# Top-32 attention on one core: the exponential moved ahead of the selection's end, and the threshold applied by a scaled Relu and a subtraction

## The chip, the cores and the metric

One core of a Trainium2 chip. TensorE (PE; PEld is its weight load), VectorE (DVE), ScalarE (ACT) and GpSimd (POOL) each run their own queue in order; SyncE (SP) issues the DMAs. The metric is the device time of one execution in microseconds, lower is better.

## The reference

```python
scores = scale * np.matmul(q, k.transpose(0, 1, 3, 2))          # 4 batches, 8 heads, 576 x 576, head size 64
kth = np.partition(scores, -top_k, axis=-1)[..., -top_k:-top_k + 1]   # top_k = 32
mask = scores >= kth
scores = np.where(mask, scores, -1000000000.0)
scores = scores - np.max(scores, axis=-1, keepdims=True)
attn = np.exp(scores)
attn = attn / (np.sum(attn, axis=-1, keepdims=True) + 1e-09)
return np.matmul(attn, v).astype(np.float32)
```

Each row of scores keeps its 32 largest entries. Two dense blocks follow for each batch: a token and channel mixing with cosine and sine, then a gated layer with a normalisation, all in float32 by three matmuls on split operands.

## The kernel before

**Attention.** The 4 x 4 pairs of heads are cut into 144 tiles of 128 query rows by 576 keys; two tiles make a group (G = 2), so there are 72 groups. For each tile `scores` makes the score tile in PSUM (`ps_s`, L449) and ScalarE copies it into `x` (L453; three group buffers). `topk` then works on a group on VectorE alone: four tensor_tensor steps with two tensors each (L468 max, L469 min, twice: 288 columns of both tiles, then 144) narrow the row, MAX8 at L472 takes the losers' best, and four rounds of MAX8 (L478) and MATCH_REPLACE8 (L481) give the 32 largest in `mx`. Round 0 gives the row maximum, `mx[..., 0]`; round 3 gives the 32nd, `mx[..., 31]`. A compare (L485, `flags`) records rows in which the narrowing may have lost an entry.

**The threshold.** ScalarE puts -max/8 into `cf` (L489) and |32nd| times a small number (L490), VectorE forms the threshold from it in one scalar_tensor_tensor of 128 x 2 (L491). `weigh` has ScalarE make `sg` = sign(score - threshold) (L500), then `x` = exp((score - max)/8) in place (L501), and GpSimd multiplies them into `sg` in pieces of 288 columns (L89, four for a group). TensorE transposes `sg` into `ps_t` (L511), ScalarE takes Relu of that into `ptb` (L512), which removes the negative entries, and `values` multiplies with V (`ps_v`, L522 to L536). A column of ones in V gives the row sum.

**What else runs.** From about 0 to 300 us the weights of the dense blocks are converted (VectorE L163 to L165, ScalarE, GpSimd `w_f`, `w_hi`); from about 300 us the dense blocks of batches 0 to 2 (`ps_m`, L572 to L574; their other operations go through a helper and stand at L588 or L89) are laid between the attention's instructions; the dense block of batch 3 runs after the attention's end.

**Order.** The Python loop emits `topk` of group g, then `weigh`, `transpose` and `values` of group g - 1. A scheduler that plans by priorities and its own estimates fixes the order of each engine's queue from that; buffers have fixed counts (`x` 3, `sg` 2, `mm` 1). A buffer's new writer waits for its last reader: `sg` of group g for the transposes of group g - 2.

Of the kernel before, what the change touches and what calls it, by code (L numbers as in the profile page):

```python
# [10 lines left out]
F32 = mybir.dt.float32  # L11
F32R = mybir.dt.float32r
I32 = mybir.dt.int32
AF = mybir.ActivationFunctionType
OP = mybir.AluOpType
# [1 line left out]
NEG = -3.0e38  # L17
MAGIC = 12582912.0
TURN = 6.283185
ULP = 1.25 * 2.0 ** -24  # L20
LN_EPS = 1e-6


# [1 line left out]
def sparse_attention_then_moe_kernel(  # L25
# [21 lines left out]
    B, H, D, S = qT.shape  # L47
# [4 lines left out]
    G = 2  # L52
# [38 lines left out]
    pool = Pieces()  # L91
# [244 lines left out]
    def run(exact):  # L336
# [93 lines left out]
            nc.sync.dma_start(extra[p, 0:D], v[b, 2 * j + 1, r])  # L430

        GATE = {}
        X, SG, MX, PT = {}, {}, {}, {}
        PER = NP * NT

        def scores(n):
# [17 lines left out]

        def topk(g):

            x = X[g]
            mx = att.tile([128, G, 32], F32, name="mx")
            mm = att.tile([128, G, S], F32, name="mm", bufs=1)
            if exact:  # L460
                src, mr = ([t[:, i] for i in range(G)] for t in (x, mm))
            else:


                z = att.tile([128, G, QUARTER + 16], F32, name="z", bufs=1)
                for t, lo, mid, hi, win in ((x, 0, HALF, S, mm), (mm, 0, QUARTER, HALF, z)):
                    a, b = t[:, :, lo:mid], t[:, :, mid:hi]
                    dve.tensor_tensor(win[:, :, 0:mid], a, b, op=OP.max)  # L468
                    dve.tensor_tensor(mm[:, :, mid:hi], a, b, op=OP.min)  # L469
                for k, losers in enumerate((slice(LOSERS, S), slice(QUARTER, LOSERS))):  # L470
                    for i in range(G):
                        dve.max(out=z[:, i, QUARTER + 8 * k:QUARTER + 8 * k + 8], in_=mm[:, i, losers])  # L472
                src = [z[:, i] for i in range(G)]
                mr = [mm[:, i, 0:QUARTER + 16] for i in range(G)]
            for r in range(4):
                top = [mx[:, i, 8 * r:8 * r + 8] for i in range(G)]
                for i in range(G):
                    last = dve.max(out=top[i], in_=src[i])  # L478
                if r < 3:
                    for i in range(G):  # L480
                        dve.match_replace(out=mr[i], in_to_replace=top[i], in_values=src[i], imm_value=NEG)  # L481
                    src = mr
            kth = mx[:, :, 31]
            if not exact:
                dve.tensor_tensor(flags[:, g], z[:, :, QUARTER + 7::8], mx[:, :, 31:32].to_broadcast([128, G, 2]),  # L485
                                  op=OP.is_gt)

            cf = att.tile([128, G, 3], F32, name="cf", bufs=3)
            act.activation(cf[:, :, 0], mx[:, :, 0], AF.Copy, scale=-0.125)  # L489
            act.activation(cf[:, :, 1], kth, AF.Abs, scale=ULP)  # L490
            dve.scalar_tensor_tensor(cf[:, :, 2], cf[:, :, 1], 1e-37, kth, op0=OP.max, op1=OP.subtract)  # L491
            MX[g] = cf
            GATE[g] = last.ins

        def weigh(n):
            x, cf = X[n // G][:, n % G], MX[n // G][:, n % G]
            if n % G == 0:
                SG[n // G] = att.tile([128, G, S], F32, name="sg", bufs=2)
            sg = SG[n // G][:, n % G]
            act.activation(sg, x, AF.Sign, bias=cf[:, 2:3])  # L500
            act.activation(x, x, AF.Exp, bias=cf[:, 0:1], scale=0.125)  # L501
            pool.tensor_tensor(sg, x, sg, op=OP.mult)

        def transpose(n):
            x = SG[n // G].rearrange("p i n -> p (i n)")
            pt = psum.tile([128, 5, 128], F32, name="ps_t")
            ptb = att.tile([128, 5, 128], F32, name="ptb", bufs=2)
            k = (5, 4)[n % G]
# [584 lines left out]
```

## Time and profile before

| | |
|---|---|
| median of 3 runs | 989.75 us (989.65 to 991.41) |
| the profiled execution | 992.02 us, its span 990.2 us |
| busy, share of the span | PE 88%, DVE 83%, ACT 64%, POOL 60% |
| granted TensorE clock, mean | 0.901 of 2.4 GHz |

The busy time of PE counts matmuls that overlap in the pipeline. The chain that ended last has PE on 43%, DVE on 26%, ACT on 10%, DMA on 9% and POOL on 6% of the span.

### The profile page before, as it was taken

Reading aid. Unit: us, or ns where it says so; the run is one execution under the profiler, and the core shown is the slowest. Engines: PE = TensorE matmul, PEld = TensorE weight load, DVE = VectorE, ACT = ScalarE, POOL = GpSimd, SP = SyncE. Lnnn points to the kernel's source line nnn. Section 1 sums busy time; section 2 is a strip of 40 time slices with the busy share of each in tenths; the row PEclk is TensorE's granted clock in tenths of the full one; section 3 lists DMA queues with packets and bytes.
Section 4 is the critical chain, followed back from the end, with each engine's and each line's share of the span. In section 5 each row is a group of like instructions: output and inputs, shape, how many; then the busy total and the mean of one; then the engine's idle time right before and its main releaser. Section 6 shows DMA issues by size and latency. Waiting matters only on the chain.

```text
span 990.2 us, 18081 instructions
## 1 busy us (share of the span) xinstructions
PE 867.8 (88%) x5802; PEld 797.5 (81%) x5802; DVE 823.0 (83%) x2710; ACT 638.0 (64%) x1319; POOL 598.7 (60%) x753
## 2 busy tenths in 40 slices
PE   4657686678779799989999999999989999999997
PEld 2546575667669798888889998898889998889987
DVE  6999999999998897889999998999998981363552
ACT  5566676779858566877776777777966775350121
POOL 2798876686956755594767666676584564421030
PEclk9955556679779699999999999899999999999999
DMA  7797665545817633744362753552743554441221
GB/s 218 215 305 227 215 210 179 145 145 186 261 60 199 230 95 106 229 143 126 110 206 60 229 160 78 218 129 95 205 160 91 201 188 166 191 168 62 104 85 52
DMA packets 79395, 159.78 MB, mean 161 GB/s; under 512 B 36143, under 2 KB 40239, under 8 KB 71866
## 3 DMA queue, kind: packets, MB, share of 16 engines
q1 hardware_dynamic: 79290, 158.53, 50.5%
q8 instruction: 48, 0.79, 0.3%
q14 instruction: 57, 0.47, 0.2%
HBM read 108.63 MB, written 23.32 MB: 133 GB/s over the span
## 4 chain that ended last, share of the span: by engine, by line
PE 43%; DVE 26%; ACT 10%; DMA 9%; POOL 6%; issue 4%; SPq 2%; ACTq 0%; POOLq 0%; DVEq 0%
PE ps_m L574 9%; PE ps_m L572 9%; PE ps_m L573 9%; PE ps_v L533 7%; DVE mm L469 4%; PE ps_s L449 4%; PE ps_t L511 4%; DVE mm L481 4%; DVE mx L478 4%; DVE z L472 2%; DVE mm L468 2%; DMA raw<-in_q_dram 2%; DMA q<-hi 2%; ACT sg L500 1%; POOL sg L89 1%
## 5 line engine op out<-in xcount | busy, mean ns | idle before, releaser
L89 POOL TENSOR_TENSOR sg<-x,sg 128x288 f32<-128x288 f32 x288 | 238.5, 857 | 141.0 <-ACT x L501 94.2
L511 PE MATMUL ps_t<-ident,sg 128*128 128x128 f32 x648 | 140.9, 314 | 60.7 <-POOL sg L89 37.5
L533 PE MATMUL ps_v<-vc,ptb 128*128 128x65 f32 (+1 forms) x1280 | 183.5, 281 | 4.7 <-ACT ptb L512 4.7
L533 PEld LDWEIGHTS ps_v<-vc,ptb 128*128 128x128 f32 (+1 forms) x1280 | 174.7, 206 | 13.6 <-ACT ptb L512 6.7
L511 PEld LDWEIGHTS ps_t<-ident,sg 128*128 128x128 f32 x648 | 97.8, 171 | 77.6 <-POOL sg L89 51.2
L500 ACT ACTIVATE sg<-x,cf 128x576 f32<-128x576 f32 x144 | 103.8, 768 | 44.2 <-DVE cf L491 43.3
L478 DVE MAX8 mx<-mm 128x8 f32<-128x160 f32 x432 | 118.8, 312 | 0.0
L453 ACT ACTIVATE x<-ps_s 128x576 f32<-128x576 f32 x144 | 92.6, 643 | 35.9 <-PE ps_s L449 32.3
L512 ACT ACTIVATE ptb<-ps_t 128x640 f32<-128x640 f32 (+1 forms) x144 | 92.7, 644 | 29.8 <-PE ps_t L511 28.2
L501 ACT ACTIVATE x<-x,cf 128x576 f32<-128x576 f32 x144 | 107.9, 767 | 0.1
L449 PE MATMUL ps_s<-k,q 128*128 128x288 f32 x256 | 91.3, 368 | 16.2 <-DVE q L369 8.6
L572 PE MATMUL ps_m<-w_t,zah 128*128 128x288 f32 (+2 forms) x272 | 98.9, 364 | 6.6 <-DVE F L588 4.8
L574 PE MATMUL ps_m<-w_t,zal 128*128 128x288 f32 (+2 forms) x272 | 97.5, 360 | 0.6 <-POOL zal L89 0.5
L573 PE MATMUL ps_m<-w_t,zah 128*128 128x288 f32 (+2 forms) x272 | 96.7, 356 | 0.0
L472 DVE MAX8 z<-mm 128x8 f32<-128x312 f32 (+1 forms) x288 | 89.6, 372 | 2.0
L572 PE MATMUL ps_m<-w_t,zbh 128*128 128x288 f32 x288 | 85.7, 302 | 2.3 <-DMA w_t<-d_sph 1.0
L481 DVE MATCH_REPLACE8 mm<-mx,mm 128x160 f32<-128x160 f32 x288 | 86.8, 308 | 0.0
L573 PE MATMUL ps_m<-w_t,zbh 128*128 128x288 f32 x288 | 86.2, 303 | 0.0
L574 PE MATMUL ps_m<-w_t,zbl 128*128 128x288 f32 x288 | 84.9, 302 | 1.2 <-POOL zbl L89 1.2
L449 PE MATMUL ps_s<-kl,q 128*128 128x288 f32 x256 | 82.9, 334 | 0.0
L468 DVE TENSOR_TENSOR mm<-x 128x576 f32<-128x576 f32 x72 | 67.7, 941 | 17.5 <-ACT x L453 16.4
L89 POOL TENSOR_TENSOR raw<-raw,hi 128x288 fp32r<-128x288 f32 x60 | 56.2, 956 | 40.2 <-ACT hi L393 40.0
(174 smaller groups left out, 2438.9 us busy)
## 6 DMA issues: line engine op xcount, KB each, us to landing
k<-hi SPq DMA_DIRECT2D x60, 144.0 KB, 2.5
kl<-raw SPq DMA_DIRECT2D x60, 144.0 KB, 2.6
vc<-in_v_dram SPq DMA_DIRECT2D x48, 128.0 KB, 2.9
w_t<-d_trh SPq DMA_DIRECT2D x4, 1152.0 KB
w_t<-d_trl SPq DMA_DIRECT2D x4, 1152.0 KB
out_dram<-t SPq DMA_DIRECT2D x32, 144.0 KB, 2.5
raw<-in_q_dram SPq DMA_DIRECT2D x15, 288.0 KB, 3.0
q<-hi SPq DMA_DIRECT2D x30, 144.0 KB, 3.3
```

Of the source, the lines that this page charges most:

```text
L89: nc.gpsimd.tensor_tensor(out[:, lo:hi], a[:, lo:hi], b[:, lo:hi], op=op)
L449: pe.matmul(o, q, k[:, m], start=a == 0, stop=a == len(terms) - 1)
L472: dve.max(out=z[:, i, QUARTER + 8 * k:QUARTER + 8 * k + 8], in_=mm[:, i, losers])
L478: last = dve.max(out=top[i], in_=src[i])
L481: dve.match_replace(out=mr[i], in_to_replace=top[i], in_values=src[i], imm_value=NEG)
L500: act.activation(sg, x, AF.Sign, bias=cf[:, 2:3])
L501: act.activation(x, x, AF.Exp, bias=cf[:, 0:1], scale=0.125)
L511: pe.transpose(pt[:, c, :], x[:, lo:lo + 128], ident)
L533: pe.matmul(o, pt[:, c, q], chunks[:, c, slot], start=alone and c == 0, stop=not alone and i == 1 and c == 3)
L572: pe.matmul(out, ah, bh, start=first, stop=False)
L573: pe.matmul(out, ah, bl, start=False, stop=False)
L574: pe.matmul(out, al, bh, start=False, stop=last)
```

## The change

Two things move. The exponential no longer waits for the 32nd largest: after round 0 of `topk`, ScalarE forms `most` = -max/8 and writes exp((score - max)/8) of both tiles into a new tile `e`, which takes the two buffers that `sg` had. After round 3 ScalarE alone forms `kth` = 2^64 times the 32nd; `weigh` then makes `x` = relu(2^64 (32nd - score)) in place, and GpSimd subtracts it from `e`, in the same pieces as the product before. An entry below the 32nd becomes hugely negative and is removed by the Relu behind the transposes, as before. The sign and VectorE's scalar_tensor_tensor at L491 are gone, and the small Abs on ScalarE with them.

```diff
@@ topk
                     last = dve.max(out=top[i], in_=src[i])
+                if r == 0:
+                    most = att.tile([128, G], F32, name="most", bufs=3)
+                    e = att.tile([128, G, S], F32, name="e", tag="sg", bufs=2)
+                    act.activation(most, mx[:, :, 0], AF.Copy, scale=-0.125)
+                    for i in range(G):
+                        act.activation(e[:, i], x[:, i], AF.Exp, bias=most[:, i:i + 1], scale=0.125)
+                    E[g] = e
...
-            cf = att.tile([128, G, 3], F32, name="cf", bufs=3)
-            act.activation(cf[:, :, 0], mx[:, :, 0], AF.Copy, scale=-0.125)
-            act.activation(cf[:, :, 1], kth, AF.Abs, scale=ULP)
-            dve.scalar_tensor_tensor(cf[:, :, 2], cf[:, :, 1], 1e-37, kth, op0=OP.max, op1=OP.subtract)
-            MX[g] = cf
             GATE[g] = last.ins
+            MX[g] = att.tile([128, G], F32, name="kth", bufs=3)
+            act.activation(MX[g], mx[:, :, 31], AF.Copy, scale=LACK)
@@ weigh
-            act.activation(sg, x, AF.Sign, bias=cf[:, 2:3])
-            act.activation(x, x, AF.Exp, bias=cf[:, 0:1], scale=0.125)
-            pool.tensor_tensor(sg, x, sg, op=OP.mult)
+            act.activation(x, x, AF.Relu, bias=kth, scale=-LACK)
+            pool.tensor_tensor(e, e, x, op=OP.subtract)
```

The scheduler lays the queues anew. In the changed file L483 is `most`, L485 the exponential, L496 `kth`, L502 the Relu; VectorE's steps stand at L469, L470, L473, L479, L489 and L492, the transposes at L512 and their Relu at L513.

VectorE, group 12, from its round 3 to the next group's narrowing (`w_f` is a weight's conversion). Before:

```order
L478 MAX mx<-mm 128x8 x2
L163 TENSOR_SCALAR w_f<-w_raw 128x512
L468 TENSOR_TENSOR mm<-x 128x2x288
L469 TENSOR_TENSOR mm<-x 128x2x288
L485 TENSOR_TENSOR flags<-z,mx 128x4
L164 SCALAR_TENSOR_TENSOR w_f<-w_raw,w_f 128x512
L491 SCALAR_TENSOR_TENSOR cf<-cf,mx 128x2
L468 TENSOR_TENSOR z<-mm 128x2x144
```

After:

```order
L479 MAX mx<-mm 128x8 x2
L163 TENSOR_SCALAR w_f<-w_raw 128x512
L469 TENSOR_TENSOR mm<-x 128x2x288
L470 TENSOR_TENSOR mm<-x 128x2x288
L492 TENSOR_TENSOR flags<-z,mx 128x4
L164 SCALAR_TENSOR_TENSOR w_f<-w_raw,w_f 128x512
L469 TENSOR_TENSOR z<-mm 128x2x144
```

One instruction is gone, which stood behind two tensor_tensor steps of the next group; the rest kept its place.

ScalarE, the same group 12, from the row maximum on. Before:

```order
L489 ACTIVATE cf<-mx 128x2
L393 ACTIVATE hi<-raw 128x576
L490 ACTIVATE cf<-mx 128x2
L512 ACTIVATE ptb<-ps_t 128x640
L453 ACTIVATE x<-ps_s 128x576
L500 ACTIVATE sg<-x,cf 128x576 x2
L501 ACTIVATE x<-x,cf 128x576
L166 ACTIVATE w_raw<-w_raw 128x512
L211 ACTIVATE w_f<-w_f 128x512
L501 ACTIVATE x<-x,cf 128x576
```

After:

```order
L483 ACTIVATE most<-mx 128x2
L485 ACTIVATE e<-x,most 128x576 x2
L496 ACTIVATE kth<-mx 128x2
L502 ACTIVATE x<-x,kth 128x576 x2
L513 ACTIVATE ptb<-ps_t 128x512
L453 ACTIVATE x<-ps_s 128x576
```

Both exponentials now stand between round 0 and round 3, and both Relus directly behind `kth`.

ScalarE in the stage with dense work (`zah` and L588/L589 are the dense block's), from group 49's row maximum on. Before:

```order
L489 ACTIVATE cf<-mx 128x2
L512 ACTIVATE ptb<-ps_t 128x640
L588 ACTIVATE zah<-F 128x288
L453 ACTIVATE x<-ps_s 128x576
L490 ACTIVATE cf<-mx 128x2
L393 ACTIVATE hi<-raw 128x576
L588 ACTIVATE zah<-F 128x288
L500 ACTIVATE sg<-x,cf 128x576
L512 ACTIVATE ptb<-ps_t 128x512
L500 ACTIVATE sg<-x,cf 128x576
```

After (the two Relus that come first are group 48's):

```order
L483 ACTIVATE most<-mx 128x2
L502 ACTIVATE x<-x,kth 128x576 x2
L453 ACTIVATE x<-ps_s 128x576
L589 ACTIVATE zah<-F 128x288
L496 ACTIVATE kth<-mx 128x2
L547 ACTIVATE xr<-ps_v 128x130
L513 ACTIVATE ptb<-ps_t 128x640
L589 ACTIVATE zah<-F 128x288
L453 ACTIVATE x<-ps_s 128x576
L589 ACTIVATE zah<-F 128x288
L513 ACTIVATE ptb<-ps_t 128x512
L485 ACTIVATE e<-x,most 128x576 x2
```

Here the exponentials stand behind `kth`, after the copy-out of the transposes that free their buffer, and group 48's Relus stand behind group 49's row maximum.

## Rows read from the trace of the kernel before

**Rows 1.** Stretches: length, busy us (count) of PE, PEld, DVE, ACT, POOL; clock, DMA, GB/s.

```profile
0.00:300.00 300.00, 211.29 (x1064) 181.36 (x1065) 284.31 (x861) 208.51 (x415) 212.89 (x270) 0.72 0.64 197
300.00:820.00 520.00, 495.35 (x3635) 465.30 (x3634) 470.44 (x1675) 381.54 (x805) 344.05 (x430) 0.97 0.49 154
820.00:990.20 170.20, 161.20 (x1107) 150.81 (x1105) 68.26 (x175) 47.90 (x100) 41.77 (x54) 0.99 0.33 121
```

**Rows 2.** The page's chain that ended last, by engine.

```profile
PE 43%; DVE 26%; ACT 10%; DMA 9%; POOL 6%; issue 4%; SPq 2%; ACTq 0%; POOLq 0%; DVEq 0%
```

**Rows 3.** L491 alone in the same stretches: busy us (count), clock, DMA share, GB/s.

```profile
0.00:300.00 300.00, 8.05 (x23) 0.72 0.64 197
300.00:820.00 520.00, 13.63 (x49) 0.97 0.49 154
```

**Rows 4.** Groups by line and form: count, busy us, mean ns, idle before, its releasers.

```profile
L491 DVE SCALAR_TENSOR_TENSOR cf<-cf,mx 128x2 f32<-128x2 f32 x72 | 21.7, 301 | 2.8 <-ACT cf L490 2.6
L501 ACT ACTIVATE x<-x,cf 128x576 f32<-128x576 f32 x144 | 107.9, 767 | 0.1
L500 ACT ACTIVATE sg<-x,cf 128x576 f32<-128x576 f32 x144 | 103.8, 768 | 44.2 <-DVE cf L491 43.3 <-PE ps_t L511 0.5
L89 POOL TENSOR_TENSOR sg<-x,sg 128x288 f32<-128x288 f32 x288 | 238.5, 857 | 141.0 <-ACT x L501 94.2 <-issue 36.6 <-PE ps_s L449 7.7
L89 POOL TENSOR_TENSOR pl<-F,ph 128x288 fp32r<-128x288 f32 x52 | 44.0, 858 | 44.8 <-ACT ph L588 27.2 <-DVE ph L588 17.2 <-issue 0.2
```

**Rows 5.** Timeline around 109 us, all engines: start us, us, engine, line, operation, operands.

```profile
109.37 2.65 POOL L89 TENSOR_TENSOR raw<-raw,hi 128x288 fp32r<-128x288 f32 x2
...
111.29 0.75 DVE L491 SCALAR_TENSOR_TENSOR cf<-cf,mx 128x2 f32<-128x2 f32 x1
...
111.96 0.45 DVE L468 TENSOR_TENSOR z<-mm 128x288 f32<-128x288 f32 x1
```

**Rows 6.** VectorE's timeline near 540 us, the same columns.

```profile
537.50 1.36 DVE L468 TENSOR_TENSOR mm<-x 128x576 f32<-128x576 f32 x1
...
540.05 0.15 DVE L491 SCALAR_TENSOR_TENSOR cf<-cf,mx 128x2 f32<-128x2 f32 x1
540.12 0.45 DVE L468 TENSOR_TENSOR z<-mm 128x288 f32<-128x288 f32 x1
```

**Rows 7.** Timeline of an early group, all engines.

```profile
93.84 1.12 PE L511 MATMUL ps_t<-ident,sg 128*128 128x128 f32 x4 [0.79 <-ACT ptb L512]
...
102.91 0.54 DVE L478 MAX8 mx<-z 128x8 f32<-128x160 f32 x2
...
112.07 1.44 ACT L500 ACTIVATE sg<-x,cf 128x576 f32<-128x576 f32 x2 [1.19 <-DVE cf L491]
```

**Rows 8.** Timeline of a group in the stage with dense work, all engines.

```profile
568.22 0.54 DVE L478 MAX8 mx<-z 128x8 f32<-128x160 f32 x2
...
572.34 0.60 PE L511 MATMUL ps_t<-ident,sg 128*128 128x128 f32 x4
...
575.09 1.45 ACT L500 ACTIVATE sg<-x,cf 128x576 f32<-128x576 f32 x2 [0.24 <-DVE cf L491]
...
577.81 2.34 POOL L89 TENSOR_TENSOR sg<-x,sg 128x288 f32<-128x288 f32 x3 [0.74 <-ACT x L501]
```

**Rows 9.** Waits (us in total, times, longest): ACT, whole span; PE, 550 to 820 us.

```profile
ACT cf L490 <- DVE mx L478: 22.6, 21, 2.7
...
PE ps_t L511 <- POOL sg L89: 2.6, 3, 1.7
```

**Rows 10.** L468, then L469, from 0 to 300 us: busy us, count.

```profile
0.00:300.00 300.00, 39.01 (x49) 0.72 0.64 197
...
0.00:300.00 300.00, 41.16 (x48) 0.72 0.64 197
```

**Rows 11.** VectorE's timeline: an early wide step and a late narrow one.

```profile
130.28 0.75 DVE L468 TENSOR_TENSOR mm<-x 128x576 f32<-128x576 f32 x1
...
575.45 0.95 DVE L469 TENSOR_TENSOR mm<-mm 128x288 f32<-128x288 f32 x1
```

More of the change, by code (lines that the diff above doesn't have):

```diff
@@ L19 @@
 TURN = 6.283185
-ULP = 1.25 * 2.0 ** -24
+LACK = 2.0 ** 64
 LN_EPS = 1e-6
@@ L432, in run @@
         GATE = {}
-        X, SG, MX, PT = {}, {}, {}, {}
+        X, E, MX, PT = {}, {}, {}, {}
         PER = NP * NT
@@ L482, in topk @@
                     src = mr
-            kth = mx[:, :, 31]
             if not exact:
@@ L486, in topk @@
                                   op=OP.is_gt)
-            cf = att.tile([128, G, 3], F32, name="cf", bufs=3)
-            act.activation(cf[:, :, 0], mx[:, :, 0], AF.Copy, scale=-0.125)
-            act.activation(cf[:, :, 1], kth, AF.Abs, scale=ULP)
-            dve.scalar_tensor_tensor(cf[:, :, 2], cf[:, :, 1], 1e-37, kth, op0=OP.max, op1=OP.subtract)
-            MX[g] = cf
             GATE[g] = last.ins
+            MX[g] = att.tile([128, G], F32, name="kth", bufs=3)
+            act.activation(MX[g], mx[:, :, 31], AF.Copy, scale=LACK)
         def weigh(n):
[L496 to L499, printed above, removed]
-            act.activation(sg, x, AF.Sign, bias=cf[:, 2:3])
-            act.activation(x, x, AF.Exp, bias=cf[:, 0:1], scale=0.125)
-            pool.tensor_tensor(sg, x, sg, op=OP.mult)
+            x, e, kth = X[n // G][:, n % G], E[n // G][:, n % G], MX[n // G][:, n % G:n % G + 1]
+            act.activation(x, x, AF.Relu, bias=kth, scale=-LACK)
+            pool.tensor_tensor(e, e, x, op=OP.subtract)
         def transpose(n):
-            x = SG[n // G].rearrange("p i n -> p (i n)")
+            x = E[n // G].rearrange("p i n -> p (i n)")
             pt = psum.tile([128, 5, 128], F32, name="ps_t")
```

## The prediction

> **What bounds the kernel now.** I first read the busy time by stage [rows 1]: three stages with three limits. Up to 300 us VectorE is busy 284.3 of 300, and so it is as good as full (some of the rest is the start); PE has 89 us to spare. From 300 to 820 us PE is busy 495 of 520 and VectorE 470 of 520: nearly a tie. From 820 us on only the last dense block runs, PE 161 of 170; attention is over, and nothing there changes but its start. Then the chain by engine [rows 2]: VectorE holds 26% of the span although it is busy for 83% of it, so about a third (0.31) of what it does decides anything, and more in the first stage. Then the groups [rows 4] and the timelines of one group in each stage [rows 7, 8], to see what waits for the threshold.
>
> A saved microsecond on VectorE is worth one up to 300 us and about 0.31 between 300 and 820 us. That is the yardstick below.
>
> **The change part by part.**
>
> *ScalarE's large steps.* Out go 144 signs of 768 ns and in come 144 Relus of the same form (a per-row bias and a scale, 128x576, SBUF to SBUF); the 144 exponentials of 767 ns stay, with `e` as the output [rows 4]. The small copies become two a group where there were two (L489, L490). Change in busy time: 0. The trace has no Relu of this form, but the sign and the exponential differ by 1 ns, so I take 768 ns; one nanosecond each way is 0.1 us in all.
>
> *GpSimd.* 288 products of 857 ns become 288 subtractions on the same shapes; the subtraction `pl` of the same size takes 858 ns [rows 4]. Change: 0.
>
> *L491 leaves VectorE.* 72 instructions, 21.7 us busy, mean 301 ns [rows 4], 23 of them up to 300 us (8.05 us) and 49 later (13.63 us) [rows 3]. The mean hides two cases. In one it shows 0.15 us and the next instruction starts 0.07 us after it [rows 6]; in the other it lasts 0.75 us and ends at 112.04, just when a GpSimd piece ends at 112.02 [rows 5]: it was held until that piece was done. So the price of taking it away lies between 0.07 us (if the next two-tensor instruction is held in its place) and the mean, 0.30 us. I take 0.2 us, the middle, because L468 behind it in rows 5 runs its short 0.45 us only after the piece had ended: part of the hold would pass on, part not, as GpSimd is idle for 29% of this stage [rows 1] and then nothing is there to hold. First stage: 23 x 0.2 = 4.6 us. Second: 49 x 0.2 x 0.31 = 3.0 us. Bounds: 23 x 0.07 + 49 x 0.07 x 0.31 = 2.7 us, and 8.05 + 13.63 = 21.7 us if all of it is on the path everywhere.
>
> The Trainium skill has the hold as a rule (SBUF — State Buffer, Terms): the port pair that VectorE and GpSimd share is locked for a whole instruction, and the loser "fully blocks". The trace agrees in the end times of rows 5. By that rule alone a hold is not abolished but handed to the next two-tensor instruction; the sum would then be the lower bound, which is the second rival below.
>
> *The wait for L491.* ScalarE's queue stood idle 43.3 us in front of the signs [rows 4], everything queued behind them (copies out of PSUM, splits) included. `kth` replaces L490 with the same wait for round 3, 22.6 us [rows 9], and `most` replaces L489 and its wait for round 0. So 43.3 us of ScalarE idling goes. ScalarE is busy 70% and 73% of the two stages [rows 1] and has little on the chain (10%, rows 2), so I price it at 0; what it hands on is that the copies of `x` come earlier, and VectorE hardly waits for them.
>
> *The exponential moves ahead.* In the first stage the buffer is free: the transposes of the group before last end at 94.96, round 0 ends at 103.45 [rows 7], and the order of the queues has both exponentials ahead of `kth` in the first 29 groups, where none was before. The threshold's way to GpSimd is shorter there by two exponentials, 1.5 us, and the hop over VectorE. But VectorE is the bound, and a group's weighing is one group behind it, so this latency is covered by the next group's `topk`, which takes longer (a group of the second stage takes 520/49 = 10.6 us): 0. In the second stage it does not happen. Round 0 ends at 568.76, the transposes that free the buffer at 572.94, and the sign started at 575.09 [rows 8]; `e` has the same two buffers, so the exponential cannot start before 572.94, 4 us after the maximum is known, and the queues show it behind `kth` in 40 of 72 groups. The sign already sat 2 us behind that limit. The way is shorter by those 2 us at most, and PE hardly waits for GpSimd there, 2.6 us in three places from 550 to 820 us [rows 9]: 0. If that cover is gone, it costs nothing more than now.
>
> *Moved with it.* The moved steps issue no DMA, and SP has the same transfers, in an order that differs here and there; in the first stage GpSimd's weight splits now stand between whole groups of four pieces instead of pairs. I price both at 0, with 3 us either way (the longest single waits in rows 9 are 1.7 and 2.7 us) for queues laid anew.
>
> **Sum.** 4.6 + 3.0 = 7.6 us less. The profiled execution, 992.0 us, becomes 984.4; it stood 2.3 us above the median of the runs, so against the median 989.75 - 7.6 = 982 us. Its own range, with the 3 us, is 977 to 987.
>
> **The rivals.**
>
> 1. *All of L491 counts.* If VectorE bounds the second stage too, its 13.63 us count fully: 989.75 - 21.7 = 968 us. For it: VectorE is 90% busy there [rows 1]. Against: PE is 95% busy.
>
> 2. *The hold passes on.* GpSimd's pieces are as many as before; each catches the next two-tensor step instead. 989.75 - 2.7 = 987 us, at the edge of no change. For it: the end times in rows 5. Against: GpSimd's idle time.
>
> 3. *The pieces land on the narrowing (slower).* In 28 of the first 29 groups the first Relu now stands at most three places behind `kth`, so the four pieces start 1 to 2 us after round 3, when VectorE is in the four two-tensor steps of the next group; before, the product started past them, at 577.81 [rows 8] behind the narrow step of 575.45 [rows 11]. Free, the wide steps take 0.75 us [rows 11]; under GpSimd 1.36 [rows 6], and the narrow ones 0.45 and 0.95 [rows 5, 11]. Fully held a group pays 2 x 1.36 + 2 x 0.95 = 4.62 us; the first stage pays (39.01 + 41.16)/24 = 3.34 now [rows 10]. The whole difference is 24 x 1.28 = 31 us, all of it on the path, so a quarter of it eats the gain. Half of it: 989.75 + 15 - 7.6 = 997 us. For it: the order. Against: GpSimd is 71% busy there and its weight splits fill the same stretch already, so that pieces mostly change places. The Trainium skill's rule on the port pair, above, is the same mechanism.
>
> 4. *A new wait at the head of ScalarE's queue.* In 24 groups the second Relu stands behind the next group's `most`, and waits for its round 0. At the mean of the present waits for round 3, 22.6/21 = 1.08 us, that is 26 us of idling where 43.3 went; if 0.31 of it reaches the end, 8 us, and the gain is gone: 990 us, no change.
>
> **How the numbers follow.** Forecast 0.40, rival 1 0.18, rival 2 0.20, rival 3 0.15, rival 4 0.07. Bounds of 0.2%, 2 us, are what a measurement of this kernel can tell from no change. Faster: forecast, rival 1 and half of rival 2, 0.68. Same: the other half of rival 2 and most of rival 4, 0.15. Slower: rival 3 and the rest, 0.17. The range reaches from rival 1's 968 less the 3 us of a new order, rounded up to 966, to rival 3's 997: about 0.08 lies below and as much above.
>
> **What would show it.** L491's row gone and VectorE's busy time down by 15 to 22 us, most of it where GpSimd is idle: the step is right. The tensor_tensor lines L469 and L470 of the changed kernel above 80 us up to 300 us, or the busy time not lower: rival 3, or 2. `e` waiting for transposes in the second stage while `kth` stands far ahead of its Relu: the buffer limit is right. A wait of Relu or `ptb` for `most` above 20 us: rival 4. The second stage, now ending before 820 us, ending more than 12 us earlier: rival 1. What would make me wrong most likely is the weight of 0.31, which is a share of the chain and no property of the edit.

## The result and the profile after

The changed kernel takes 994.79 us (median of 7 runs, 989.13 to 997.55), the kernel before 989.65 in the same comparison: a ratio of 1.0051, 95% interval 1.0028 to 1.0074. It is half a per cent slower; I had forecast 982 us, faster. Ratios use the executions in the faster of two states, and so does e12's time below, which leaves one execution out. The profiled execution has a span of 993.7 us. "Two-input steps" below are VectorE's four tensor_tensor instructions that narrow a group's rows.

The same views as [rows 1] and [rows 2], of the changed kernel: stretches with length, busy us (count) of PE, PEld, DVE, ACT, POOL; clock, DMA, GB/s; then the page's busy line and its chain by engine.

```profile
0.00:300.00 300.00, 207.93 (x1061) 177.01 (x1062) 272.01 (x831) 211.13 (x415) 211.40 (x268) 0.73 0.65 196
300.00:820.00 520.00, 493.19 (x3615) 463.10 (x3614) 486.53 (x1633) 377.86 (x801) 357.07 (x428) 0.97 0.51 155
820.00:993.70 173.70, 164.75 (x1130) 154.12 (x1128) 68.34 (x175) 50.15 (x104) 44.78 (x57) 1.00 0.31 118
...
PE 865.9 (87%) x5802; PEld 794.2 (80%) x5802; DVE 826.9 (83%) x2638; ACT 639.1 (64%) x1319; POOL 613.2 (62%) x753
...
PE 37%; DVE 32%; ACT 9%; POOL 7%; DMA 7%; issue 4%; SPq 1%; DVEq 0%; POOLq 0%; ACTq 0%
```

L491 is gone, and VectorE is 12.3 us less busy up to 300 us (272.0 against 284.3, at 30 instructions fewer). But from 300 to 820 us it is 16.1 us busier (486.5 against 470.4) with 42 instructions fewer. Something there became slower. It is the two-input steps and the pieces of GpSimd. The groups by line and form (count, busy us, mean ns, idle before, its releasers) that answer to [rows 4]:

```profile
L89 POOL TENSOR_TENSOR e<-e,x 128x288 f32<-128x288 f32 x288 | 264.9, 949 | 132.7 <-ACT x L502 67.1 <-issue 52.2 <-PE ps_t L512 6.1
L502 ACT ACTIVATE x<-x,kth 128x576 f32<-128x576 f32 x144 | 105.9, 770 | 0.6
L485 ACT ACTIVATE e<-x,most 128x576 f32<-128x576 f32 x144 | 103.8, 769 | 0.5
```

The Relu costs what the sign did (770 against 768 ns), and ScalarE's idling in front of the weighing, 43.3 us before, is 1.1 us. (It idles elsewhere instead: its busy time is 639.1 us, 638.0 before, in a span that is 3.5 us longer.) A piece takes 949 ns on average where it took 857 [rows 4]. L469 and then L470 of the changed kernel (they are L468 and L469 of before), up to 300 us and from 300 to 820, and behind them L468 and L469 of before in the second stretch; the first stretch answers to [rows 10]:

```profile
0.00:300.00 300.00, 39.15 (x48) 0.73 0.65 196
300.00:820.00 520.00, 78.74 (x96) 0.97 0.51 155
...
0.00:300.00 300.00, 38.32 (x48) 0.73 0.65 196
300.00:820.00 520.00, 86.35 (x96) 0.97 0.51 155
```

```profile
300.00:820.00 520.00, 69.19 (x96) 0.97 0.49 154
...
300.00:820.00 520.00, 74.23 (x96) 0.97 0.49 154
```

In the first stage the steps cost 77.5 us, 2.7 less than before. In the second they cost 165.1 where they cost 143.4: 21.7 us more, as much as L491 took in the whole kernel. Why can be seen in one group. VectorE, ScalarE, GpSimd and one row of PE around group 45 of the changed kernel (start us, us, engine, line, operation):

```profile
537.44 0.56 DVE L479 MAX8 mx<-mm 128x8 f32<-128x160 f32 x2
537.67 4.13 POOL L89 TENSOR_TENSOR e<-e,x 128x288 f32<-128x288 f32 x4 [3.11 <-ACT x L502]
...
538.69 0.20 ACT L496 ACTIVATE kth<-mx 128x2 f32<-128x2 f32 x1
538.79 1.07 DVE L469 TENSOR_TENSOR mm<-x 128x576 f32<-128x576 f32 x1
539.79 1.36 DVE L470 TENSOR_TENSOR mm<-x 128x576 f32<-128x576 f32 x1
540.99 0.60 PE L512 MATMUL ps_t<-ident,e 128*128 128x128 f32 x4
541.07 1.05 DVE L469 TENSOR_TENSOR z<-mm 128x288 f32<-128x288 f32 x1
...
544.84 0.20 ACT L483 ACTIVATE most<-mx 128x2 f32<-128x2 f32 x1 [2.36 <-DVE mx L479]
544.95 0.58 ACT L513 ACTIVATE ptb<-ps_t 128x512 f32<-128x512 f32 x1
...
545.43 1.43 ACT L485 ACTIVATE e<-x,most 128x576 f32<-128x576 f32 x2
...
546.76 0.77 ACT L502 ACTIVATE x<-x,kth 128x576 f32<-128x576 f32 x1
547.66 4.40 POOL L89 TENSOR_TENSOR e<-e,x 128x288 f32<-128x288 f32 x4 [4.89 <-issue]
```

Round 3 of group 45 ends at 538.0. Its exponentials run at 545.4, its pieces at 547.7, 9.7 us after round 3. The buffer for the exponentials is free when the transposes end at 541.6; but the next group's `most` stands ahead of them in ScalarE's queue, and ScalarE idles 2.36 us in front of it, until that group's round 0 is done. The pieces come so late that they lie on the steps of the group after the next: the pieces at 537.7 are group 44's, and under them group 46's wide steps take 1.07 and 1.36 us instead of 0.75, and the narrow one 1.05 instead of 0.45 ([rows 11], [rows 5] for the free ones). By the timeline, 75 of the 192 steps from 300 to 820 us lie under pieces of the group before the last one; before, it was 16 of 191.

### The profile page after: what moved, and what is told of

It reads as the page before. It is cut to its first block, busy times and chain, and to the rows that moved or that the text cites. A ratio compares the mean times of both kernels' runs of the same rounds, so it can differ in the third digit from the quotient of the medians.

```text
span 993.7 us, 17998 instructions
## 1 busy us (share of the span) xinstructions
PE 865.9 (87%) x5802; PEld 794.2 (80%) x5802; DVE 826.9 (83%) x2638; ACT 639.1 (64%) x1319; POOL 613.2 (62%) x753
## 4 chain that ended last, share of the span: by engine, by line
PE 37%; DVE 32%; ACT 9%; POOL 7%; DMA 7%; issue 4%; SPq 1%; DVEq 0%; POOLq 0%; ACTq 0%
PE ps_m L573 8%; PE ps_m L575 8%; PE ps_m L574 8%; PE ps_v L534 5%; DVE mm L470 5%; DVE mx L479 5%; DVE mm L489 5%; POOL e L89 4%; DVE z L473 4%; DVE mm L469 3%; PE ps_t L512 3%; PE ps_s L449 3%; DVE z L469 2%; ACT e L485 2%; DVE F L589 2%
## 5 line engine op out<-in xcount | busy, mean ns | idle before, releaser
L89 POOL TENSOR_TENSOR e<-e,x 128x288 f32<-128x288 f32 x288 | 264.9, 949 | 132.7 <-ACT x L502 67.1
L534 PEld LDWEIGHTS ps_v<-vc,ptb 128*128 128x128 f32 (+1 forms) x1280 | 173.1, 205 | 21.7 <-ACT ptb L513 14.4
L512 PE MATMUL ps_t<-ident,e 128*128 128x128 f32 x648 | 138.7, 309 | 42.6 <-POOL e L89 31.5
L512 PEld LDWEIGHTS ps_t<-ident,e 128*128 128x128 f32 x648 | 94.6, 168 | 60.2 <-POOL e L89 42.7
L449 PE MATMUL ps_s<-k,q 128*128 128x288 f32 x256 | 91.0, 367 | 33.5 <-ACT x L453 24.8
L479 DVE MAX8 mx<-mm 128x8 f32<-128x160 f32 x432 | 119.4, 318 | 0.0
L513 ACT ACTIVATE ptb<-ps_t 128x640 f32<-128x640 f32 (+1 forms) x144 | 92.7, 644 | 35.1 <-PE ps_t L512 34.5
L502 ACT ACTIVATE x<-x,kth 128x576 f32<-128x576 f32 x144 | 105.9, 770 | 0.6
L485 ACT ACTIVATE e<-x,most 128x576 f32<-128x576 f32 x144 | 103.8, 769 | 0.5
L473 DVE MAX8 z<-mm 128x8 f32<-128x312 f32 (+1 forms) x288 | 89.9, 371 | 1.9
L449 PEld LDWEIGHTS ps_s<-k,q 128*128 128x128 f32 x256 | 56.3, 220 | 40.8 <-ACT x L453 32.3
L489 DVE MATCH_REPLACE8 mm<-mx,mm 128x160 f32<-128x160 f32 x288 | 87.7, 314 | 0.0
L573 PE MATMUL ps_m<-ph,w_t 128*128 128x288 f32 x256 | 77.8, 305 | 1.4 <-DVE mx L479 0.6
```

What stands on the lines that cost most here:

```text
L89: nc.gpsimd.tensor_tensor(out[:, lo:hi], a[:, lo:hi], b[:, lo:hi], op=op)
L449: pe.matmul(o, q, k[:, m], start=a == 0, stop=a == len(terms) - 1)
L485: act.activation(e[:, i], x[:, i], AF.Exp, bias=most[:, i:i + 1], scale=0.125)
L502: act.activation(x, x, AF.Relu, bias=kth, scale=-LACK)
L512: pe.transpose(pt[:, c, :], x[:, lo:lo + 128], ident)
L534: pe.matmul(o, pt[:, c, q], chunks[:, c, slot], start=alone and c == 0, stop=not alone and i == 1 and c == 3)
```

## The experiments

The theories that the expectations name: **A**, the pieces land on the two-input steps; **C**, the early exponential needs `e`'s buffer early and holds up ScalarE's queue, so that score tiles are freed late; **D**, the new layout of the queues by itself. The scheduler lays all queues anew after any edit, so each run has some of D in it.

For all runs I worked out from the timeline, as for group 45 above, the **lag**: the mean time from the end of round 3 to the group's first piece, for groups 29 to 49 and 50 to 71; and the time for a group in the same halves (the end of round 3 of group 49 less that of 28, by 21, and of 71 less that of 49, by 22). "PE not busy" is the span less PE's busy time on the page. All columns but the ratio come from one profiled execution, which can lie some us off the run's median (e7 and e8 4.2 us above, e17 3.6 above, e18 3.5 below).

| run | ratio to before (95%) | PE busy | PE not busy | lag, us | us for a group |
|---|---|---|---|---|---|
| before | 1 | 867.8 | 122.4 | 7.6 / 6.7 | 10.74 / 10.27 |
| after | 1.0051 (1.0028 to 1.0074) | 865.9 | 127.8 | 9.6 / 8.5 | 10.60 / 10.51 |
| e1 | 0.9980 (0.9956 to 1.0004) | 862.0 | 123.8 | 7.4 / 7.0 | 10.27 / 10.70 |
| e2 | 0.9887 (0.9846 to 0.9927) | 864.0 | 115.2 | 4.9 / 5.0 | 10.02 / 10.13 |
| e3 | 1.0054 (1.0027 to 1.0081) | 862.9 | 127.5 | 7.9 / 5.4 | 10.59 / 9.71 |
| e4 | 0.9889 (0.9868 to 0.9910) | 861.0 | 116.0 | 5.0 / 4.9 | 9.96 / 10.03 |
| e5 | 0.9967 (0.9944 to 0.9991) | 863.6 | 121.6 | 7.4 / 8.4 | 10.20 / 10.56 |
| e6 | 0.9982 (0.9962 to 1.0001) | 859.3 | 124.0 | 8.5 / 9.0 | 10.22 / 10.53 |
| e7 | 0.9909 (0.9881 to 0.9938) | 867.3 | 115.9 | 5.1 / 4.9 | 10.11 / 10.06 |
| e8 | 0.9977 (0.9952 to 1.0002) | 863.2 | 125.7 | 8.0 / 7.0 | 10.48 / 10.61 |
| e11 | 0.9935 (0.9910 to 0.9960) | 860.4 | 117.1 | 6.4 / 6.3 | 10.03 / 10.19 |
| e12 | 0.9956 (0.9934 to 0.9979) | 866.3 | 118.1 | 6.1 / 5.1 | 10.46 / 9.89 |
| e13 | 0.9924 (0.9894 to 0.9953) | 856.3 | 124.8 | 7.6 / 9.0 | 9.90 / 10.61 |
| e14 | 1.0045 (1.0022 to 1.0069) | 862.2 | 129.3 | 9.7 / 8.4 | 10.65 / 10.47 |
| e15 | 0.9979 (0.9957 to 1.0001) | 863.4 | 123.5 | 7.5 / 6.8 | 10.71 / 10.25 |
| e16 | 1.0021 (1.0002 to 1.0039) | 862.4 | 129.1 | 7.3 / 9.1 | 10.75 / 10.98 |
| e17 | 1.0017 (0.9999 to 1.0034) | 874.4 | 119.3 | 5.0 / 6.9 | 10.31 / 10.44 |
| e18 | 1.0132 (1.0108 to 1.0156) | 862.7 | 134.3 | 2.6 / 3.0 | 10.62 / 10.02 |

**The threshold step alone, and the late exponential.** e2 is the kernel before without L490 and L491, a single copy of -32nd in their place (the 32nd entry then gets weight 0). e1 is the changed kernel with the exponential back in `weigh`.

```diff
# e2, from before
-            act.activation(cf[:, :, 1], kth, AF.Abs, scale=ULP)
-            dve.scalar_tensor_tensor(cf[:, :, 2], cf[:, :, 1], 1e-37, kth, op0=OP.max, op1=OP.subtract)
+            act.activation(cf[:, :, 2], kth, AF.Copy, scale=-1.0)
# e1, from after
-                        act.activation(e[:, i], x[:, i], AF.Exp, bias=most[:, i:i + 1], scale=0.125)
...
+            act.activation(e, x, AF.Exp, bias=MO[n // G][:, n % G:n % G + 1], scale=0.125)
             act.activation(x, x, AF.Relu, bias=kth, scale=-LACK)
```

> The changed kernel with the exponential back behind the threshold: it is issued in weigh, straight ahead of the Relu, and takes its buffer there; the rest of the change stays (no L491, Relu, subtraction). Theory A (the early exponential, which waits for its buffer in the queue, puts GpSimd's pieces on the next group's narrowing): the narrowing goes from 165 us between 300 and 820 us back to 145 to 150 us, and the time is 980 to 988 us. Rival B (the Relu and the subtraction, or the new layout of the queues as such, cost the time): narrowing 160 us or more, 993 to 997 us.

> The kernel before with L491 and the Abs taken out: ScalarE gives minus the 32nd largest as the sign's bias, so that the 32nd entry itself gets weight 0 (that part of the computation is left out). It measures what the lost step alone is worth. My step in the prediction says 7.6 us less than before, 982 us; if a held instruction only hands its wait on, 2 to 3 us, 987 us; if the step is worth nothing because PE bounds, 990 us.

e2 took 980.26 us, 9.4 less than before (7 to 15 by the interval of the ratio): in this layout taking L491 away is worth that. e1 took 987.65. With the exponential back in `weigh` 7 us of the changed kernel's time are gone, but most of the gain is still missing, and the two-input steps cost 155.3 us from 300 to 820 us, between the numbers of both theories. Part of the loss seems to go with the move; one pair of layouts does not show how much.

**Pieces kept off the two-input steps.** e3 is the changed kernel with one more GpSimd instruction of 128x1 that reads the result of the next group's narrowing; the pieces stand behind it.

```diff
+            if n % G == 0 and n // G + 1 in NARROW:
+                GO[n // G] = nc.gpsimd.tensor_scalar(tick[:, 0:1], NARROW[n // G + 1][:, 0, 0:1], 1.0, 0.0,
+                                                      op0=OP.mult, op1=OP.add).ins
+                with tc.issue_after(GO[n // G]):
+                    pool.tensor_tensor(e, e, x, op=OP.subtract)
```

> The changed kernel with GpSimd's four pieces of a group held until the next group's narrowing is over: one GpSimd instruction of 128x1 that reads the narrowing's last result stands ahead of them in its queue. Theory A (pieces on the narrowing): the narrowing falls from 165 us between 300 and 820 us to under 140 us and the time to 980 to 990 us, although every product comes later. Rival C (the pieces end too late, x is freed late, and ScalarE and PE wait for it, 30 and 25 us in the changed kernel): these waits grow by 20 us or more and the time goes to 998 us or above.

VectorE's busy time fell from 826.9 to 803.6 us, the two-input steps from 300 to 820 us from 165.1 to 146.4, and nothing was won: 994.05 us. GpSimd now stands in front of the gate. Its waits (us in total, times, longest):

```profile
POOL tick L507 <- DVE mm L472: 68.0, 33, 5.2
```

Shorter two-input steps did not bring the time back here. As GpSimd's other work also waits behind the gate, this run alone does not settle theory A.

**The arithmetic without the move.** e4 is the kernel before with a Relu in the sign's place and a subtraction for the product; the exponential stays behind it, in place.

```diff
-            act.activation(cf[:, :, 1], kth, AF.Abs, scale=ULP)
-            dve.scalar_tensor_tensor(cf[:, :, 2], cf[:, :, 1], 1e-37, kth, op0=OP.max, op1=OP.subtract)
+            act.activation(cf[:, :, 2], kth, AF.Copy, scale=LACK)
-            act.activation(sg, x, AF.Sign, bias=cf[:, 2:3])
+            act.activation(sg, x, AF.Relu, bias=cf[:, 2:3], scale=-LACK)
             act.activation(x, x, AF.Exp, bias=cf[:, 0:1], scale=0.125)
-            pool.tensor_tensor(sg, x, sg, op=OP.mult)
+            pool.tensor_tensor(sg, x, sg, op=OP.subtract)
```

> The kernel before with only the arithmetic of the change: a Relu of 2^64 (32nd - score) in the sign's place and into the same tile, the exponential behind it in place as before, a subtraction for the product, and L490 and L491 replaced by one small copy on ScalarE. The exponential is not moved. If the change loses by moving the exponential (theories A and C), this is as fast as the kernel with the threshold step left out, 980 us (977 to 984). If Relu and subtraction themselves are at fault, it is near the kernel with the late exponential, 987 us, or slower. If any new layout of the queues moves the time by several us (D), it lies anywhere from 980 to 990.

It takes 978.32 us (977.53 to 978.84), 1.1% less than before: the best of all, and it computes what the changed kernel computes. So Relu and subtraction need not cost anything. The same place in the program as group 45 above; round 3 ends at 533.5, the pieces start 2.9 us later, when the next group's steps are nearly over, and the steps of this group run free (over the whole stretch they cost 148.3 us, no less than before):

```profile
532.98 0.55 DVE L478 MAX8 mx<-mm 128x8 f32<-128x160 f32 x2
...
534.07 0.75 DVE L468 TENSOR_TENSOR mm<-x 128x576 f32<-128x576 f32 x1
534.15 1.43 ACT L499 ACTIVATE sg<-x,cf 128x576 f32<-128x576 f32 x2
534.74 0.74 DVE L469 TENSOR_TENSOR mm<-x 128x576 f32<-128x576 f32 x1
...
535.41 0.45 DVE L468 TENSOR_TENSOR z<-mm 128x288 f32<-128x288 f32 x1
535.48 0.77 ACT L500 ACTIVATE x<-x,cf 128x576 f32<-128x576 f32 x1
535.89 0.46 DVE L469 TENSOR_TENSOR mm<-mm 128x288 f32<-128x288 f32 x1
536.38 3.11 POOL L89 TENSOR_TENSOR sg<-x,sg 128x288 f32<-128x288 f32 x4 [2.25 <-issue]
```

PE waits for score tiles that ScalarE copies out (before, the changed kernel, e4):

```profile
PE ps_s L449 <- ACT x L453: 8.1, 12, 1.4
```

```profile
PE ps_s L449 <- ACT x L453: 24.8, 21, 2.6
```

```profile
PE ps_s L449 <- ACT x L453: 9.7, 9, 3.5
```

**One half, one step.** e5 has the early exponential in groups 0 to 28 only (`if g < 29`), e6 in groups 29 to 71 only. e7 is e4 with the row maximum's small copy at round 0; e8 is e4 with the exponential ahead of the Relu, each writing the tile that the other wrote.

```diff
# e8, from e4
-            act.activation(sg, x, AF.Relu, bias=cf[:, 2:3], scale=-LACK)
-            act.activation(x, x, AF.Exp, bias=cf[:, 0:1], scale=0.125)
-            pool.tensor_tensor(sg, x, sg, op=OP.subtract)
+            act.activation(sg, x, AF.Exp, bias=cf[:, 0:1], scale=0.125)
+            act.activation(x, x, AF.Relu, bias=cf[:, 2:3], scale=-LACK)
+            pool.tensor_tensor(sg, sg, x, op=OP.subtract)
```

> The changed kernel with the early exponential in groups 0 to 28 only (the first stage, where its buffer is free); groups 29 to 71 have the exponential in weigh, ahead of the Relu. Late everywhere took 987.7 us, early everywhere 994.8. If the loss is made in the second stage (the narrowing's steps are slow there, and the exponential waits for its buffer there), this is near 988 us. If it is made in the first stage (PE's dense work is already behind at 300 us), near 995 us.

> The other half: the early exponential in groups 29 to 71 only, groups 0 to 28 with the exponential in weigh. If the loss is made in the second stage, near 995 us, with the narrowing's means up by 50 to 100 ns from 300 to 560 us as in the changed kernel. If it is made in the first, near 988 us. Both halves near 988 or both near 995 would mean that the layout of the queues, not the early exponential, makes the difference.

> The kernel with the Relu in the sign's place (978.3 us) and only the small copy of the row maximum moved up to round 0, as the change has it. Between that kernel and the late exponential (987.7 us) lie two steps, this one and the order of exponential and Relu. If the copy at round 0 makes ScalarE wait where other work stands behind it (my rival 4), this is near 988 us; if not, 978 us, and the order of the two large steps makes the 9 us. A third value is the size of what a new layout of the queues alone does.

> The other of the two steps alone: the kernel with the Relu in the sign's place (978.3 us), with the exponential ahead of the Relu in weigh, so that the GpSimd pieces follow the Relu and not the exponential; the copy of the maximum stays at the end of topk. If the place of the pieces in time matters (theory A), near 988 us, with the narrowing's sum near the late exponential's and well above 226 us; if the copy at round 0 does it, 978 us.

986.87, 986.45, 980.84 and 986.50 us. The copy at round 0 is not it (2.5 us, within the intervals). With the two large steps on ScalarE in the other order the kernel is 8 us slower; that this is the price of the order is not shown, because e17 below loses more than that against e4 by a layout alone. Against the late exponential (e1, 987.65 us) early in either half costs nothing; only both together lose 8 us, which no theory of one stage explains. By what was expected of e6, both halves near 988 speak for the layout and not for the early exponential. And e6 has the late pieces (8.5 and 9.0 us) and the dear steps (163.3 us from 300 to 820 us) of the changed kernel, and is as fast as e5.

**Without pieces.** e9 is the kernel before without the product, e10 the changed kernel without the subtraction; the last step of ScalarE writes the tile that is transposed. In e10 the factor of 2^64 is 1 as well, so that the two kernels transpose different numbers.

```diff
# e9, from before
-            act.activation(x, x, AF.Exp, bias=cf[:, 0:1], scale=0.125)
-            pool.tensor_tensor(sg, x, sg, op=OP.mult)
+            act.activation(sg, x, AF.Exp, bias=cf[:, 0:1], scale=0.125)
# e10, from after
-LACK = 2.0 ** 64
+LACK = 1.0
...
-            act.activation(x, x, AF.Relu, bias=kth, scale=-LACK)
-            pool.tensor_tensor(e, e, x, op=OP.subtract)
+            act.activation(e, x, AF.Relu, bias=kth, scale=-LACK)
```

> The kernel before without the GpSimd product: the last ScalarE step of a group writes the tile that TensorE transposes, and so the result isn't masked. Its partner is the changed kernel without the subtraction. Without pieces nothing lands on the narrowing: 0.4 to 0.7 of the 20 us that VectorE's two-input steps lose to the pieces now, and a shorter way, so 960 to 980 us.

> The changed kernel without the GpSimd subtraction, the Relu writing the tile that is transposed (the result isn't masked). Theory A, that the change loses by its pieces landing on the narrowing: without pieces it is faster than its partner by what L491 is worth, 8 to 11 us. Theory C, that the early exponential holds up ScalarE's queue at its buffer, and so the freeing of the score tiles: it is not faster than its partner by more than 3 us, with a wait of PE for x above 20 us.

958.97 and 964.04 us: without pieces the changed kernel is not the faster one (5 us behind, with intervals that overlap: 0.9713, 0.9678 to 0.9748, and 0.9744, 0.9709 to 0.9778), against A's number. C's wait isn't there either: PE waits 12.9 us for x, where e9 waits 22.9. The busy lines of the page, e9 and then e10, show what is:

```profile
PE 846.4 (88%) x5802; PEld 785.3 (82%) x5802; DVE 764.1 (80%) x2710; ACT 638.4 (67%) x1319; POOL 355.6 (37%) x465
```

```profile
PE 862.1 (89%) x5802; PEld 795.9 (83%) x5802; DVE 755.5 (78%) x2638; ACT 644.9 (67%) x1319; POOL 343.0 (36%) x465
```

PE is not busy for 111.6 and 102.2 us, 9.4 less in e10; but its same 5802 matmuls take 15.7 us longer, at a mean granted clock of 0.901 instead of 0.920. The pair doesn't decide: a slower PE in a stage that others bound also fills its own waits.

**The buffer.** e11 is e7 with a small copy at round 0 into `sg` itself, which needs that buffer as early as the early exponential does; e12 makes the same copy into a tile of its own.

```diff
+                    SG[g] = att.tile([128, G, S], F32, name="sg", bufs=2)              # e11
+                    act.activation(SG[g][:, :, 0], mx[:, :, 0], AF.Copy, scale=-0.125)
+                    act.activation(spare, mx[:, :, 0], AF.Copy, scale=-0.125)          # e12
```

> The kernel with the Relu in the sign's place and the row maximum's copy at round 0 (980.8 us), and one more small ScalarE copy (128x2) at round 0 that writes into the buffer of sg, so that ScalarE needs that buffer as early as the early exponential does; the exponential itself isn't moved. If it is the buffer that makes the change lose (it must be free sooner, and ScalarE's queue stands until it is), this is at 986 us or above, with a longer way from round 3 to the pieces and PE waiting for x above 18 us. If not, it is as fast as its partner with the same copy into a tile of its own.

> The partner: the same additional small copy at round 0 into a tile of its own with three buffers, which waits for nothing else. 72 small copies on an engine that is idle a third of the time: 980.8 us, within 2 us.

981.19 and 983.60 us. Needing the buffer early costs nothing against the partner, and PE waits 12.1 us for score tiles, below the 18 that C asked for: C is not borne out. The partner, which should have done nothing, is slower than e7 by 0.5% of the time (ratios 0.9956 and 0.9909, whose intervals just touch): a first sign that a layout by itself can be worth more than the 3 us I had allowed. (A third buffer for `e`, the direct test, was not tried.)

**The same steps, laid anew.** e13 is the changed kernel with Relu and pieces preferred by the scheduler; e14 has the early exponential written behind round 0's MATCH_REPLACE; e15 is the kernel before with L489 at round 0.

```diff
# e13, from after
+            with tc.high_priority(offset=500):
                 act.activation(x, x, AF.Relu, bias=kth, scale=-LACK)
                 pool.tensor_tensor(e, e, x, op=OP.subtract)
```

> The changed kernel with the same steps, where the scheduler is told to prefer the Relu and the GpSimd pieces, which lays all queues anew. If the early exponential itself costs the time, 992 to 997 us, unless the Relu comes sooner and takes the pieces off the next narrowing; if this one layout of the queues was bad luck, anywhere from 985 to 995.

> The changed kernel with the early exponential written behind round 0's MATCH_REPLACE in the program, not ahead of it: the same steps, a small change of order. If the early exponential itself costs the time, 992 to 997 us; if the layout does, anywhere from 985 to 995.

> The kernel before with only the small copy of the row maximum (L489) moved up to round 0, as the change has it: the threshold step L491 and the sign stay. If layouts scatter by no more than 3 us, 987 to 993; a value outside tells how much a layout can do by itself.

984.35, 993.53 and 988.63 us. e13 has every step of the changed kernel and is faster than before, by 0.8%. So the change's work need not make the kernel slower; an order of it does. Nor do the pieces on the two-input steps decide the time. e13's L469 and L470 from 300 to 820 us:

```profile
300.00:820.00 520.00, 78.01 (x96) 0.99 0.50 156
...
300.00:820.00 520.00, 85.37 (x96) 0.99 0.50 156
```

That is 163.4 us, 20.0 more than before and almost the 165.1 of the changed kernel, which takes 10 us longer.

**Is it the lag?** In groups 29 to 49 e13's lag is 2 us shorter than the changed kernel's, and a group takes 9.9 us instead of 10.6. e16 prefers sign, exponential and product in the kernel before, e17 the three steps in e4, and e18 adds the transposes and their copy-out to e13's preference.

> The kernel before with the scheduler told to prefer sign, exponential and product; the steps are the same. Before, the pieces start 7.6 and 6.7 us after round 3 in groups 29 to 49 and 50 to 71, and a group takes 10.7 and 10.3 us. If the pieces' lateness sets the time for a group, the two move together: below 6 us and under 10.2 us, or above 8 us and over 10.5 us. Time 980 to 995 us accordingly; no change of either, 989 us.

> The kernel with the Relu in the sign's place, the same preference for Relu, exponential and subtraction. There the pieces start 5.0 and 4.9 us after round 3 and a group takes 10.0 us in both halves. They have little left to gain: 976 to 982 us if the pieces stay below 6 us, more if they come later.

> The changed kernel with the preference for Relu and pieces, and for the transposes and their copy-out too, which free the exponential's buffer. With the first preference alone it took 984.4 us, with the pieces 7.6 us behind round 3 and 9.9 us for a group in groups 29 to 49, and 9.0 and 10.6 us in groups 50 to 71. If lateness sets the time and the buffer's release was part of it, the second half falls below 7 us and 10.3 us too, and the time to 976 to 983 us; if the transposes' preference only moves other work, 984 to 990 us.

992.36, 991.90 and 1002.29 us. In e16 lag and time for a group moved together (9.1 us and 10.98 in the second half), and in e17's second half too; its first half has e4's lag, 5.0 us, and a group takes 10.31 all the same. e18 has the shortest lag, and 3.0 us and 10.02 us in its second half, as was expected of it; and yet it is the slowest. Its pieces start while the next group's steps run:

```profile
539.90 0.54 DVE L479 MAX8 mx<-mm 128x8 f32<-128x160 f32 x2
...
540.55 0.75 DVE L469 TENSOR_TENSOR mm<-x 128x576 f32<-128x576 f32 x1
540.71 1.44 ACT L503 ACTIVATE x<-x,kth 128x576 f32<-128x576 f32 x2
541.59 0.75 DVE L470 TENSOR_TENSOR mm<-x 128x576 f32<-128x576 f32 x1
541.62 4.10 POOL L89 TENSOR_TENSOR e<-e,x 128x288 f32<-128x288 f32 x4 [4.09 <-issue]
542.25 1.06 DVE L469 TENSOR_TENSOR z<-mm 128x288 f32<-128x288 f32 x1
543.35 0.94 DVE L470 TENSOR_TENSOR mm<-mm 128x288 f32<-128x288 f32 x1
```

So the lag is no law, and neither is the time for a group: in e18 the last round 3 ends at 795.9 us, 13.9 sooner than in the changed kernel, and more dense work is left. That is where the end is made in nearly all runs: PE's dense matmuls that are left at 820 us (busy us and count of `ps_m` from there on; before, after, e4, e18). Only e16 is slow with little left (151.9 us, as in e5); its attention ends last of all, at 854.5 us. Before, it ends at 838.2, and not ahead of 820 as the prediction has it.

```profile
820.00:1010.00 190.00, 155.65 (x1046) 0.99 0.30 108
```

```profile
820.00:1010.00 190.00, 159.25 (x1069) 0.99 0.29 108
```

```profile
820.00:1010.00 190.00, 146.89 (x1006) 0.98 0.26 99
```

```profile
820.00:1010.00 190.00, 166.54 (x1114) 0.99 0.29 109
```

And the same matmuls up to 300 us (before, after, e4):

```profile
0.00:300.00 300.00, 46.25 (x193) 0.72 0.64 197
```

```profile
0.00:300.00 300.00, 42.30 (x188) 0.73 0.65 196
```

```profile
0.00:300.00 300.00, 46.69 (x229) 0.74 0.65 198
```

Of the 63 dense matmuls by which the changed kernel is behind e4 at 820 us, 41 are missing at 300 us already. In that stage its pieces come 4.3 us after round 3 (groups 0 to 28; 5.9 in e4, 7.8 before), and its two-input steps cost what e4's do (77.5 and 77.3 us). Against the kernel before it is behind by 23, 5 of them at 300 us. So lateness in the second stage is no account of what it lost against e4.

## Why the prediction was wrong

**L491, 7.6 us: right in kind, perhaps too small.** Alone it is worth 9.4 us (e2; 7 to 15 by the interval), and with the change's arithmetic 11.1 (e4, 989.43 - 978.32; 9 to 13). Rival 2, that the hold passes on for 2.7 us, lies outside both intervals, and rival 1, 21.7 us, further outside on the other side. With the same 0.2 us for each, 4.6 + 9.8 x 0.31 = 7.6, and it takes 0.49 of the 9.8 in the place of 0.31 to make 9.4 (an estimate from e2 alone, whose interval allows 0.31 too). In the changed kernel the first stage's 4.6 us did not reach PE's dense work: VectorE is 12.3 us less busy there, and PE has done 188 dense matmuls by 300 us, 193 before and 229 in e4.

**The exponential moves ahead, 0: the step that failed.** I wrote that in the second stage the way to GpSimd gets shorter by up to 2 us. It got longer: the pieces start 9.6 and 8.5 us after round 3 instead of 7.6 and 6.7. I had seen that the exponential would stand behind `kth` there, as it does at 545.4. I had not asked what else stands there. The Relu, which needs nothing but `kth`, now queues behind the exponential, and both queue behind whatever ScalarE's queue has ahead of them. In groups 29 to 71 the transposes free the buffer 3.6 us after round 3 on average; the exponential starts at 5.6 and the Relu at 7.5. In 21 of the 43 groups the next group's `most` stands between `kth` and the Relu, as at 544.84 above; there the lag is 11.1 us, in the others 7.0.

The price of 0 was wrong on VectorE: pieces that come 2 us later land on the steps of another group, 21.7 us in the second stage. PE does not wait for the pieces there (0.7 us from 300 to 820 us, 5.7 before), as I had it, but it waits longer for score tiles (24.8 us in all, 8.1 before). What this is worth in time is not shown. Against e4, which has the same arithmetic, the move costs 16 us (1.0051 - 0.9889 of 990); but with the steps in `weigh` preferred, e13 against e17, it gains 9 (0.9924 against 1.0017), although e13's two-input steps cost nearly what the changed kernel's do. The step's mechanism failed; how much of the loss is its own stays open.

**Queues laid anew, 3 us either way: too small by far.** (And 982 with 3 us either way is 979 to 985, not the 977 to 987 that I gave.) This term also failed, and it is large enough for the whole miss. The changed kernel's steps took 984.4, 993.5, 994.8 and 1002.3 us in four layouts, 18 us apart, e4's 978.3 and 991.9, those of before 989.7 and 992.4 (988.6 with one small copy moved). In e17 against e4 the loss is mostly PE's own time, 874.4 us for the matmuls that take 861.0, at a mean clock of 0.893 instead of 0.911; in the changed kernel against e4 it is mostly waiting, 127.8 against 116.0. "PE not busy" sorts the runs by their steps better than the time does: 115 to 119 us for e2, e4, e7, e11, e12 and e17; 122 to 126 where the exponential stands ahead of the Relu in `weigh`, in all groups or in one half (e1, e5, e6, e8); 122 to 129 before (with e15, e16); 125 to 134 with the early exponential in all groups (e3, e13, e14, e18 and the changed kernel). From the middle of the first to the middle of the last, 116.6 to 127.8, is 11 us. The grouping is shown, on one execution each; that these 11 us are the cost of the move is not. In the changed kernel against e4 9.0 of the 11.8 us lie up to 300 us (92.1 against 83.1), ahead of the stage in which the pieces come later; e13 with 124.8 us is faster than e17 with 119.3; and without pieces the early exponential has less of it, not more (e10, 102.2, against e9, 111.6).

**Rival 3: the mechanism was there, the stage was not.** I had the pieces land on the two-input steps in the first stage, because they come sooner there. The two lines cost 77.5 us there, not above 80. They landed in the second stage, because they come later. But e13 and e6 carry them too, and e13 is faster than before and e6 no slower, so the rival's price in time is not borne out. Its price, 21.7 us on VectorE, is of the size of the 31 us that I had worked out as the most for the first stage. The rule that I cited from the Trainium skill (SBUF — State Buffer, Terms), a port pair locked for a whole instruction, agrees with 1.36 us for a step that takes 0.75 free; the pieces pay as well, 949 ns for 857.

**Rival 4: seen in part.** `most` waits 17.1 us in all, just below the 20 I had set, and it stands ahead of the late Relus in 21 groups. e7 moves that copy alone for 2.5 us, within the intervals, but without the early exponentials behind it. In e18, the slowest run, `most` waits 37.5 us, and in e13, which is fast, 18.0; so this wait does not decide the time by itself either.

**The buffer limit: right, and not the whole of the wait.** The exponential starts behind the copy-out of the transposes in the second stage, as I had it, but 2.0 us after the buffer is free on average; e11 needs the buffer as early and is no slower than its partner.

**What stays open:** which property of a layout decides. A short lag goes with a short time for a group in e2, e4, e7 and e11, and a long one with a long time in e16; but e13's first half is fast at a lag of 7.6 us, and the first halves of e17 and e18 are slow at a short one. The granted clock has a part in it that I can read but not predict. So the cause of the half per cent is open: the move under this layout, the layout by itself, or both.

## What to carry to other kernels

Price a moved step by what queues behind it on its own engine, and ask on whose steps the work that it releases will land, later as well as sooner. Where a scheduler lays the queues anew, an edit that should do nothing is a run worth having: here the same steps in other orders differ by 14 us (e4, e17) and 18 us (the changed kernel's), more than the step that was saved. And split a change into its arithmetic and its move: e4 keeps the first and is 1.1% faster than before, in one of its two layouts.

## What the runs showed of the hardware

Pieces and two-input steps slow each other: a piece took 949 ns in the changed kernel, 871 in e4 and 970 in e18; a 128x288 step under them 1.05 us instead of 0.45. And layouts differ in the granted clock: 0.893 to 0.908 in the twelve executions of e17, 0.910 to 0.916 in the four of e4, with the same steps. As many matmuls, 5802, took 846.4 us of PE at a mean granted clock of 0.920 (e9, without pieces) and 874.4 at 0.893 (e17), 28 us that no engine's wait shows. The clock of a stretch is a mean over the two levels, 1.2 and 2.4 GHz. Up to 300 us, where PE is busy for 219 of 300 us and pauses again and again, e17 was granted 0.70, e4 0.74 (e17, then e4):

```profile
0.00:300.00 300.00, 219.06 (x1060) 182.07 (x1061) 276.21 (x834) 209.14 (x410) 208.77 (x268) 0.70 0.64 195
```

```profile
0.00:300.00 300.00, 216.86 (x1104) 182.34 (x1105) 275.87 (x840) 212.96 (x419) 206.35 (x272) 0.74 0.65 198
```
